# Top-32 attention and a highway layer on one core: the 32nd score joins the maximum that gives the top score and the threshold

## The chip, the cores and the metric

The kernel runs on one core of a Trainium2 chip. A core has five engines with a queue each: TensorE (PE in the profile; PEld is its weight load), VectorE (DVE), ScalarE (ACT), GpSimd (POOL) and SyncE (SP), and 16 DMA engines that all queues share. The engines run side by side and meet at semaphores: an instruction waits at the head of its queue until what it reads has been written, and what stands behind it on that queue waits too. The metric is the device time of one execution in microseconds (us); the median of the runs counts.

## The reference, cut to what matters

Eight batches of eight heads, 576 queries and keys of 64 numbers each. Of each row of 576 scores the 32 largest stay, and the softmax goes over those; the result, with the heads side by side, goes through a highway layer.

```python
scores = scale * np.matmul(q, k.transpose(0, 1, 3, 2))          # (8, 8, 576, 576)
kth = np.partition(scores, -32, axis=-1)[..., -32:-31]
scores = np.where(scores >= kth, scores, -1000000000.0)
attn = np.exp(scores - np.max(scores, axis=-1, keepdims=True))
attn = attn / (np.sum(attn, axis=-1, keepdims=True) + 1e-09)
x = (attn @ v), heads side by side                              # (4608, 512)
H = np.maximum(x @ w_h, 0.0)
T = 1.0 / (1.0 + np.exp(-(x @ w_t + b_t)))
out = T * H + (1.0 - T) * x
```

## The kernel before, in words

**Units and pairs.** A unit is 128 rows of 576 scores: 128 queries of one head, or the last 64 queries of two heads. Two units make a pair, and there are 288 units and 144 pairs. `step(i)` is called for 143 pairs, in order; the order of the instructions on each queue is the order of the code (`manual_schedule`), written out by hand. A start (`begin`) and an end (`finish`) stand around the steps.

**How a row finds its 32nd score.** TensorE writes the scores of a pair into PSUM (`xs`). VectorE takes the eight largest of each of six segments of 96 (`segs`, L353, twelve MAX8 for a pair) into `cand`, a tile of 8 groups of 8 for each unit. `refine` (L358 to L388) narrows these 48 down. Elementwise maxima and minima of neighbouring segments (`high`, `low`, L366 and L368), a sign change (`neg`, L370), and four MAX8 over 24 (L373, L376) give two sorted lists for each unit. A joint operation on them (L378) writes eight numbers into column 1 of `cand`, and one `tensor_reduce` (L382) takes the maximum of columns 0 and 1 over the groups. The first is the row's top score, the second a threshold THR with about 24 scores above it. Both go to `wall`, a table with a row for each unit.

ScalarE then makes a mask of the scores above THR and counts them (`mask_count`, L397, count in `csum`). TensorE adds the mask to the scores in PSUM (L410), so that the scores above THR fall out, and VectorE takes the eight largest of what remains (`below`, L420, two MAX8 over 576) into `wall`. With the threshold itself these are nine numbers (NPK), of which the count tells which one is the 32nd: `hits` (L426, VectorE) sets a flag of nine for the one whose place fits the count, `pick_a` (L436, GpSimd) multiplies the flags with the nine numbers, and `pick_b` (L439, VectorE) adds the nine products, of which all but one are zero. The 32nd of a pair is stored two rows further on in `wall`, in the row of the next pair.

**What uses it.** `biases` (L391, GpSimd) turns the top score of pair i+1 and the 32nd of pair i into two biases (`be`). For the first unit of a pair ScalarE makes a filter `r` from its bias (L443), which VectorE joins with the exponentials `e` (`keep_min`, L450). For the second GpSimd compares the scores with the 32nd (`above_one`, L454), and VectorE multiplies (`keep_mul`, L460). Where GpSimd has too much to do, VectorE does both in one instruction (L465). The results `ep` are transposed by a DMA (L481), and TensorE multiplies them with the values.

**The order around the change.** In `step(i)` VectorE does: twelve `segs` of pair i+1, two `below` of pair i, `high` and `low` of pair i+1, `hits` of pair i, `neg` and the four small MAX8 of pair i+1, `pick_b` of pair i, the joint operation (L378), `keep_min` of pair i-1, the `tensor_reduce` (L382), for some steps two small instructions for the highway layer, and `keep_mul` of pair i-1. GpSimd does `above_one`, one operation of the highway layer (`do_work`), `pick_a`, then the DMAs that it issues itself, and `biases`, which is made to wait for `keep_mul`. GpSimd's DMAs are, one in most steps and two in some: an accumulating add into `s1` (`do_add`, L694), a cast of `x` into `xb` (L582), or a load of values or weights (L176 to L222). What an add or a cast fills is stored or transposed by SyncE two steps later. ScalarE's masks of pair i+1 close the step.

Of the kernel before, what the change touches and what calls it, by code (L numbers as in the profile page):

```python
# [10 lines left out]
ALU = mybir.AluOpType  # L11
FP32 = mybir.dt.float32
# [6 lines left out]
NSEG = 6  # L19
RANK = 24  # L20
ABOVE = -(1.0 + 2.0**-23)
# [5 lines left out]
def kernel(  # L27
# [10 lines left out]
    nc = tc.nc  # L38
    P = nc.NUM_PARTITIONS
# [26 lines left out]
    NU = len(units)  # L66
# [3 lines left out]
    consts = ctx.enter_context(tc.tile_pool(name="consts", bufs=1))  # L70
# [23 lines left out]
    NPK = TOP_K - RANK + 1  # L94
# [1 line left out]
    for jj in range(NPK):  # L96
        nc.vector.memset(pidx[:, jj : jj + 1], S - 2.0 * (TOP_K - jj))

    TOP, THR, KTH = 0, 1, NPK + 1
    wall = consts.tile([P, NU + 2, NPK + 2], FP32)  # L100
    fac = consts.tile([P, 2, 2], FP32)
    nc.vector.memset(fac[:, :, 0], -scale)
# [6 lines left out]
        nc.vector.memset(en[:, 0, :, 0:1], 3.0e38)  # L109
        ends.append(en)  # L110
    csum = consts.tile([P, NU], FP32)
    nc.vector.memset(wall[:, 0:2, KTH : KTH + 1], 0.0)

    def kth(u):
        return wall[:, u + 2, KTH : KTH + 1]
# [6 lines left out]

    cands = []
    for i in range(4):
        cand = consts.tile([P, 2, 8, 8], FP32, name=f"cand{i}")
        nc.vector.memset(cand[:, :, NSEG:, 0:1], -3.0e38)
        cands.append(cand)
    NM = 4
    masks = []
# [228 lines left out]
    def refine(g, cand):  # L358
        u0, u1 = pairs[g][0], pairs[g][1] + 1
        en = ends[g % NE]  # L360
        one = cand[:, :, 0:NSEG:2, :]
        two = cand[:, :, 1:NSEG:2, ::-1]
        high = cpool.tile([P, 2 * HALF], FP32, name="high")
        low = cpool.tile([P, 2 * HALF], FP32, name="low")
        neg = cpool.tile([P, 2 * HALF], FP32, name="neg")
        nc.vector.tensor_tensor(high[:].rearrange("p (s k r) -> p s k r", s=2, r=8), one, two, ALU.max)  # L366
        yield
        nc.vector.tensor_tensor(low[:].rearrange("p (s k r) -> p s k r", s=2, r=8), one, two, ALU.min)  # L368
        yield
        nc.vector.tensor_scalar(neg[:], high[:], -1.0, None, ALU.mult)  # L370
        yield
        for s in range(2):
            nc.vector.max(en[:, 0, s, 1:9], low[:, s * HALF : (s + 1) * HALF])  # L373
            yield
        for s in range(2):
            nc.vector.max(en[:, 1, s, 0:8], neg[:, s * HALF : (s + 1) * HALF])  # L376
            yield
        nc.vector.scalar_tensor_tensor(  # L378
            out=cand[:, :, :, 1], in0=en[:, 1, :, 0:8], scalar=-1.0, in1=en[:, 0, :, 0:8], op0=ALU.mult, op1=ALU.min
        )  # L380
        yield
        nc.vector.tensor_reduce(  # L382
            wall[:, u0:u1, TOP : THR + 1],
            cand[:, :, :, 0:2].rearrange("p s r k -> p s k r"),
            mybir.AxisListType.X,
            ALU.max,
        )
        yield  # L388

    def biases(g):  # L390
        return nc.gpsimd.tensor_tensor(be[:, g], wall[:, 2 * g : 2 * g + 2, TOP : KTH + 1 : KTH - TOP], fac[:], ALU.mult)  # L391

# [22 lines left out]
        return e  # L417

    def below(u, ps):
        nc.vector.max(wall[:, u, THR + 1 : KTH], ps)  # L420


    def hits(pair):
        u0, u1 = pair[0], pair[1] + 1
        hit = cpool.tile([P, 2, NPK], FP32, name="hit")
        nc.vector.tensor_tensor(  # L426
            hit[:],
            pidx[:].unsqueeze(1).to_broadcast([P, 2, NPK]),
            csum[:, u0:u1].unsqueeze(2).to_broadcast([P, 2, NPK]),
            ALU.is_equal,  # L430
        )
        return hit

    def pick_a(pair, hit):
        u0, u1 = pair[0], pair[1] + 1
        nc.gpsimd.tensor_tensor(hit[:], hit[:], wall[:, u0:u1, THR:KTH], ALU.mult)  # L436

    def pick_b(pair, hit):
        nc.vector.tensor_reduce(wall[:, pair[0] + 2 : pair[0] + 4, KTH], hit[:], mybir.AxisListType.X, ALU.add)  # L439
# [263 lines left out]
    st = {}  # L703
# [71 lines left out]
    def step(i):  # L775
        j = i - 3
        live = i < NG
        prev = 0 <= i - 1 < NG
        back = 0 <= j < NG
        nxt = i + 1 < NG  # L780
        b, k_in = divmod(i, SPB)
        last_steps = i >= NG - 8
        nb = len(stages)
        if i == 3 or nb < B and i >= (nb - 2) * SPB + 16 > 16 - 1 and not to_prep:
            stages[nb] = stage_tiles()
            todo_kq.extend(loads_kq(nb, *stages[nb]))
        if live and b + 1 < B:
            if k_in == 3:
                todo_v.extend(loads_v(b + 1, vbs[(b + 1) % 2]))
            if k_in == (1 if b else 7):  # L790
                preps[b + 1] = prep_alloc(kds[(b + 1) % 2])
                parts = [(hp, part) for hp in range(NP) for part in range(2)]
                parts[2:2] = [(0, 7), (0, 8)]
                to_prep.extend((b + 1, *part) for part in parts)
        layers.extend(ready)
        ready.clear()
        if live:
            pr = pairs[i]
            for s in range(2):
                mask_add(st[i]["ps"][s], st[i]["m"][s], s)  # L800
        if prev:
            pu, ps_ = pairs[i - 1], st[i - 1]
            ps_["r"] = [above(pu[0], ps_["sc"][0])]
            ps_["r"].append(above_one(pu[1], ps_["sc"][1]) if len(pool_work) < (3 if last_steps else 5) else None)
        if late:
            late.pop(0)()
        if back:
            back_pv(j)
            back_xs(j)
            st.pop(j)  # L810
        spare(8 if i + 2 >= NG or units[pairs[i + 2][0]][1] < nfull or po["n"] else 3)
        ev = prep_filler() if to_prep and (i <= SPB or (len(to_prep) > 15 - k_in or len(layers) > 2) and i % 2) else None
        do_work(nc.gpsimd, 2 * dm if prev and ps_["r"][1] is None else dm)
        segs(i + 1, 2 * NSEG)
        if live:
            below(pr[0], st[i]["ps"][0])
            below(pr[1], st[i]["ps"][1])
        if live:
            st[i]["e"] = [expo(pr[0], st[i]["sc"][0])]
        if nxt:  # L820
            copy_both(i + 1)
        if ev:
            ev()
        if i + 2 < NG:
            start_scores(i + 2)
        if layers and (last_steps or i <= SPB or kind[0] or not to_prep):
            kind[0] = False
            late.append(layers.pop(0)())
        elif i > SPB:
            kind[0] = True  # L830
            piece = prep_filler()
            if piece:
                late.append(piece)
        spare(4 if late else 10)
        if live:
            st[i]["e"].append(expo(pr[1], st[i]["sc"][1]))
            pass
        ra = refine(i + 1, st[i + 1]["cand"]) if nxt else iter(())

        def masked(s):  # L840
            if not prev:
                return None
            u = pu[s]
            if ps_["r"][s] is not None:
                ep, ins = (keep_min, keep_mul)[s](u, ps_["e"][s], ps_["r"][s])
            else:
                ep, ins = keep(u, ps_["sc"][s], ps_["e"][s])
            ps_["et"][s] = transposes(ep)
            return ins

        for _ in range(2):
            next(ra, None)
        if live:
            hit = hits(pr)
            pick_a(pr, hit)
        added = bool(adds or casts)
        if adds:
            do_add(i)
        elif casts:
            turns.append((i + 2, casts.pop(0)()))  # L860
        elif todo_v:
            todo_v.pop(0)()
        if todo_v and (i < 5 or added and i <= SPB):
            todo_v.pop(0)()
        for _ in range(5):
            next(ra, None)
        if live:
            pick_b(pr, hit)
        next(ra, None)
        masked(0)  # L870
        for _ in ra:
            pass
        scaling = norms.pop(0)() if norms else iter(())
        next(scaling, None)
        last = masked(1)
        if live:
            after(biases(i + 1), last)
        next(scaling, None)
        if nxt:
            masks_of(i + 1)  # L880
        while turns and turns[0][0] <= i and len(flying) < 2:
            turns.pop(0)[1]()
        while stores and stores[0][0] <= i:
            stores.pop(0)[1]()
        for _ in range(min(2, len(todo_kq))):
            todo_kq.pop(0)()
# [56 lines left out]
    def finish():  # L943
# [49 lines left out]
        hit = hits(pr)  # L993
        ep, _ = keep_min(pu[0], old["e"][0], relu)
        old["et"][0] = transposes(ep)
        nc.vector.tensor_tensor(hit[:], hit[:], wall[:, pr[0] : pr[1] + 1, THR:KTH], ALU.mult)
        pick_b(pr, hit)
        x2 = xps.tile([P, 3 * BANK], FP32, tag="x", name="xs")
        cur["et"] = [etpool.tile([P, nck, P], BF16, name="et") for s in range(2)]
# [13 lines left out]
        yb = xs_of(nfull, 0, n)  # L1013
        project(bank(x1, 0), ya["qt"], ya["xT"], wh, False)
        do_work(nc.vector, NG * dm)
        nc.vector.scalar_tensor_tensor(cond[:], wall[:, 0:NU, THR + 1], ABOVE, wall[:, 0:NU, THR], ALU.mult, ALU.add)
        while stores:
            stores.pop(0)[1]()
        sure(2, cond[:], 1.0)
# [119 lines left out]
```

## Time and profile before

| | |
|---|---|
| median of 3 runs | 806.73 us (806.29 to 807.61) |
| the profiled execution's own time | 806.17 us |
| its span, first to last instruction | 804.5 us |
| VectorE busy | 772.8 us, 96% |
| ScalarE busy | 757.2 us, 94% |
| TensorE busy | 686.7 us, 85% |
| GpSimd busy | 559.9 us, 70% |
| granted TensorE clock, mean | 0.996 |

The profile is that of one execution. A group of instructions is printed as line, engine, operation, output and inputs with their shapes, count; then the busy time in us and the mean in ns of one; then the idle time of the engine just ahead of them, and what ended it. A timeline row gives the start in us from the span's start, the duration in us, engine, line, operation, and in brackets the idle time before it with what ended it. Instructions on an engine overlap a little in the records: the next one starts before the one before it has ended, so what an instruction takes of its queue's time is the distance from its start to the next start.

### The profile page before, as it was taken

To read this page: it belongs to the slowest core of one execution; us is meant where nothing else is said; L and a number is where in the kernel's file an instruction comes from. 1 tells how busy PE (TensorE), PEld (TensorE's weight loads), DVE (VectorE), ACT (ScalarE), POOL (GpSimd) and SP (SyncE) were. 2 spreads that over 40 slices of the span, in tenths; PEclk is the share of its full clock that TensorE was granted. 3 is DMA by queue.
4 is the path that set the end of the run, shared out by engine and by line. 5 is a ranking of instruction groups with operands and counts; after the bars stand their busy time and mean duration, and the time that the engine had idled before them with its cause. 6 is when DMAs were issued, how large, how long until landed. Compare 5 with 4: busy or idle time off the path is not lost.

```text
span 804.5 us, 20583 instructions
## 1 busy us (share of the span) xinstructions
PE 686.7 (85%) x6369; PEld 494.7 (61%) x6459; DVE 772.8 (96%) x4020; ACT 757.2 (94%) x1401; POOL 559.9 (70%) x712
## 2 busy tenths in 40 slices
PE   7889998888888888888987889888888888988884
PEld 5666766566666666566665666666666566665662
DVE  5999999999999999999999999999999999999996
ACT  5999999999999999999999999999999999999984
POOL 2666867777777767777767776777776777766750
PEclk9999999999999999999999999999999999999998
DMA  6789968996799667998669766898767996555653
GB/s 121 87 137 159 134 116 140 141 143 93 140 152 148 108 96 137 154 131 125 102 135 159 125 113 107 150 156 126 112 121 136 160 124 109 90 106 110 108 90 88
DMA packets 346359, 100.37 MB, mean 125 GB/s; under 512 B 330624, under 2 KB 338432, under 8 KB 346240
## 3 DMA queue, kind: packets, MB, share of 16 engines
q1 hardware_dynamic: 291024, 79.16, 54.1%
q0 software_dynamic: 53536, 19.34, 22.6%
q8 instruction: 53, 0.87, 0.4%
q10 hardware_dynamic: 1680, 0.46, 0.3%
q14 instruction: 66, 0.54, 0.2%
HBM read 31.72 MB, written 9.44 MB: 51 GB/s over the span
## 4 chain that ended last, share of the span: by engine, by line
ACT 37%; DVE 32%; PE 23%; DMA 4%; issue 3%; SPq 1%; another core or an unknown queue 0%; DVEq 0%; ACTq 0%
ACT m L397 15%; DVE wall L420 12%; DVE cand L353 9%; ACT e L416 7%; ACT sc L348 6%; PE pso L278 5%; ACT r L443 4%; PE xs L309 4%; PE xs L326 3%; DVE ep L450 3%; DMA xT<-xb 3%; PE fp L522 3%; PE xs L410 3%; PE pso L494 2%; ACT xs L508 2%
## 5 line engine op out<-in xcount | busy, mean ns | idle before, releaser
L353 DVE MAX8 cand<-xs 128x8 f32<-128x96 f32 x1728 | 297.5, 248 | 11.4 <-PE xs L335 6.2
L278 PE MATMUL pso<-cst,ident_b 128*128 128x252 bf16 x1841 | 246.8, 272 | 42.8 <-ACT xs L508 40.4
L454 POOL TENSOR_SCALAR ro<-sc,wall 128x576 bf16<-128x576 f32 x135 | 232.8, 1724 | 0.0
L416 ACT ACTIVATE e<-sc,be 128x576 bf16<-128x576 f32 x288 | 226.5, 787 | 0.1
L278 PEld LDWEIGHTS <-ident_b 128*128 128x128 bf16 x1841 | 173.4, 98 | 81.4 <-issue 49.5
L420 DVE MAX8 wall<-xs 128x8 f32<-128x576 f32 x288 | 204.3, 751 | 5.6 <-PE xs L410 3.5
L309 PE MATMUL xs<-kT,qT 64*128 64x256 f32 x1024 | 145.3, 400 | 30.6 <-DVE high L366 26.2
L348 ACT COPY sc<-xs 128x1152 f32<-128x1152 f32 x144 | 161.0, 1118 | 0.7 <-DVE cand L353 0.6
L309 PEld LDWEIGHTS xs<-kT,qT 64*128 64x128 f32 x1024 | 93.0, 186 | 61.3 <-issue 37.6
L397 ACT ACTIVATE m<-xs,wall 128x576 int8<-128x576 f32 x144 | 107.4, 746 | 18.2 <-DVE wall L382 17.1
L436 POOL TENSOR_TENSOR hit<-hit,wall 128x18 f32<-128x18 f32 x143 | 32.4, 227 | 121.2 <-DVE hit L426 114.0
L397 ACT ACTIVATE m<-sc,wall 128x576 int8<-128x576 f32 x144 | 111.4, 773 | 0.0
L443 ACT ACTIVATE r<-sc,be 128x576 bf16<-128x576 f32 x143 | 109.9, 769 | 0.0
L410 PE MATMUL xs<-m,ident_b 128*128 128x512 bf16 (+1 forms) x512 | 92.7, 274 | 17.3 <-ACT m L397 15.2
L494 PEld LDWEIGHTS <-et 128*128 128x128 bf16 (+1 forms) x1600 | 68.6, 100 | 19.2 <-issue 3.5
L391 POOL TENSOR_TENSOR be<-wall,fac 128x4 f32<-128x4 f32 x144 | 29.2, 203 | 72.5 <-DVE ep L460 53.7
L410 PEld LDWEIGHTS <-ident_b 128*128 128x128 bf16 x576 | 51.7, 97 | 44.8 <-issue 24.1
L494 PE MATMUL pso<-vb,et 128*128 128x65 bf16 (+1 forms) x1600 | 74.4, 194 | 4.2 <-DMA et<-ep 0.3
L450 DVE TENSOR_TENSOR ep<-e,r 128x576 bf16<-128x576 bf16 x143 | 64.6, 452 | 0.2 <-ACT r L443 0.2
L318 PEld LDWEIGHTS xs<-kd,qT 128*128 128x128 f32 x256 | 38.1, 188 | 42.5 <-issue 42.1
L318 PE MATMUL xs<-kd,qT 128*128 128x128 f32 x256 | 62.5, 326 | 0.0
L460 DVE TENSOR_TENSOR ep<-e,ro 128x576 bf16<-128x576 bf16 x135 | 60.7, 449 | 0.0
(127 smaller groups left out, 1028.9 us busy)
## 6 DMA issues: line engine op xcount, KB each, us to landing
kin<-in_k_dram SPq DMA_DIRECT2D x64, 128.0 KB, 2.9
qin<-in_q_dram SPq DMA_DIRECT2D x62, 128.0 KB, 3.1
out_dram<-s SPq DMA_DIRECT2D x30, 256.0 KB, 2.8
s<-h POOLq DMA_DIRECT2D x29, 256.0 KB, 4.0
et<-ep SPq DMA_TRANSPOSE x286, 3.3
xb<-x POOLq DMA_DIRECT2D x30, 128.0 KB, 3.0
vb<-in_v_dram POOLq DMA_DIRECT2D x28, 128.0 KB, 4.8
vb<-in_v_dram POOLq DMA_DIRECT2D x24, 64.0 KB, 3.1
```

The lines of the kernel that those rows point to most:

```text
L278: nc.tensor.matmul(po["t"][:, 4 * DE : BANK], ident_b[:], cst[:, 0 : BANK - 4 * DE], start=True, stop=True, skip_group_check=True,)
L309: nc.tensor.matmul(ps[:, mo + n0 : mo + n0 + 256], qT[r : r + D, hp, qs : qs + P], kT[r : r + D, hp, n0 : n0 + 256], start=(n0 == 0), stop ...
L318: nc.tensor.matmul(ends, qT[:, hp, qs : qs + P], kd[:, hp, :], start=True, stop=True)
L348: nc.scalar.copy(sc[:], both)
L353: nc.vector.max(cand[:, s, :], sc[:, s * SEG : (s + 1) * SEG])
L397: nc.scalar.activation(m1[:].bitcast(I8)[:, 1 : 2 * S : 2], ps, AF.Sign, bias=wall[:, u, THR : THR + 1], scale=ABOVE, accum_out=csum[:, u ...
L410: nc.tensor.matmul(ps[:, s0:s1], ident_b[:], m1[:, s0:s1], start=False, stop=True, skip_group_check=True)
L416: nc.scalar.activation(e[:], sc, AF.Exp, bias=tb(u), scale=scale)
L420: nc.vector.max(wall[:, u, THR + 1 : KTH], ps)
L443: nc.scalar.activation(r[:], sc, AF.Relu, bias=eb(u), scale=BIGK)
L454: nc.gpsimd.tensor_scalar(r[:], sc, kth(u), None, ALU.is_ge)
L494: nc.tensor.matmul(pso[r0 : r0 + ql, col : col + DE], ets[s][:, c, gi * P2 : gi * P2 + ql], vb[:, h, vc, :], start=(c == 0), stop=(c == nc ...
```

## The change

The 32nd becomes a third column of the joint maximum. `cand` grows from 8 to 9 groups, and its columns are now 0 the top score, 1 the 32nd (KTH), 2 the threshold (THR). GpSimd's product of flags and numbers is written straight into column 1 of `cand` of pair i+1, and the `tensor_reduce` takes the maximum over nine groups of three columns where it took two columns over eight groups. The sum `pick_b` goes out of the step (it stays in `finish`). `wall` has its columns in the order 0 top, 1 32nd, 2 threshold, 3 to 10 the eight below.

Two things move. `hits` goes from between `low` and `neg` to behind the fourth small MAX8, and the product goes with it; and the DMAs that GpSimd issues in a step now stand ahead of the product in its queue.

```diff
-    TOP, THR, KTH = 0, 1, NPK + 1
+    TOP, KTH, THR, LOW = 0, 1, 2, 3
...
-    nc.vector.memset(wall[:, 0:2, KTH : KTH + 1], 0.0)
...
-        cand = consts.tile([P, 2, 8, 8], FP32, name=f"cand{i}")
-        nc.vector.memset(cand[:, :, NSEG:, 0:1], -3.0e38)
+        cand = consts.tile([P, 2, NPK, 8], FP32, name=f"cand{i}")
+        nc.vector.memset(cand[:, :, NSEG:, :], -3.0e38)
...
-            out=cand[:, :, :, 1], in0=en[:, 1, :, 0:8], scalar=-1.0, in1=en[:, 0, :, 0:8], op0=ALU.mult, op1=ALU.min
+            out=cand[:, :, 0:8, THR], in0=en[:, 1, :, 0:8], scalar=-1.0, in1=en[:, 0, :, 0:8], op0=ALU.mult, op1=ALU.min
...
-            wall[:, u0:u1, TOP : THR + 1],
-            cand[:, :, :, 0:2].rearrange("p s r k -> p s k r"),
+            wall[:, u0:u1, TOP:LOW],
+            cand[:, :, :, TOP:LOW].rearrange("p s r k -> p s k r"),
...
-    def pick_a(pair, hit):
-        u0, u1 = pair[0], pair[1] + 1
-        nc.gpsimd.tensor_tensor(hit[:], hit[:], wall[:, u0:u1, THR:KTH], ALU.mult)
+    def pick(pair, pen, cand):
+        nc.gpsimd.tensor_tensor(cand[:, :, :, KTH], pen[:], wall[:, pair[0] : pair[1] + 1, THR:], ALU.mult)
...
-        for _ in range(2):
-            next(ra, None)
-        if live:
-            hit = hits(pr)
-            pick_a(pr, hit)
         added = bool(adds or casts)
         if adds:
             do_add(i)
...
-        for _ in range(5):
+        for _ in range(7):
             next(ra, None)
         if live:
-            pick_b(pr, hit)
+            pick(pr, hits(pr), st[i + 1]["cand"])
         next(ra, None)
         masked(0)
```

The other lines of the diff only follow the new columns (`biases`, `below`, and `finish`).

More of the change, by code (lines that the diff above doesn't have):

```diff
@@ L390, in biases @@
     def biases(g):
-        return nc.gpsimd.tensor_tensor(be[:, g], wall[:, 2 * g : 2 * g + 2, TOP : KTH + 1 : KTH - TOP], fac[:], ALU.mult)
+        return nc.gpsimd.tensor_tensor(be[:, g], wall[:, 2 * g : 2 * g + 2, TOP:THR], fac[:], ALU.mult)
     def mask_count(u, ps):
@@ L419, in below @@
     def below(u, ps):
-        nc.vector.max(wall[:, u, THR + 1 : KTH], ps)
+        nc.vector.max(wall[:, u, LOW:], ps)
     def hits(pair):
@@ L995, in finish @@
         old["et"][0] = transposes(ep)
-        nc.vector.tensor_tensor(hit[:], hit[:], wall[:, pr[0] : pr[1] + 1, THR:KTH], ALU.mult)
+        nc.vector.tensor_tensor(hit[:], hit[:], wall[:, pr[0] : pr[1] + 1, THR:], ALU.mult)
         pick_b(pr, hit)
@@ L1015, in finish @@
         do_work(nc.vector, NG * dm)
-        nc.vector.scalar_tensor_tensor(cond[:], wall[:, 0:NU, THR + 1], ABOVE, wall[:, 0:NU, THR], ALU.mult, ALU.add)
+        nc.vector.scalar_tensor_tensor(cond[:], wall[:, 0:NU, LOW], ABOVE, wall[:, 0:NU, THR], ALU.mult, ALU.add)
         while stores:
```

## The prediction, made before the changed kernel ran

> **What bounds the kernel now.** I read the page first: the shares of the engines, the chain that ended last, the costliest groups. Then one step of VectorE and of GpSimd in the timeline, then the rows of single lines.
>
> ```profile
> PE 686.7 (85%) x6369; PEld 494.7 (61%) x6459; DVE 772.8 (96%) x4020; ACT 757.2 (94%) x1401; POOL 559.9 (70%) x712
> ACT 37%; DVE 32%; PE 23%; DMA 4%; issue 3%; SPq 1%; another core or an unknown queue 0%; DVEq 0%; ACTq 0%
> L353 DVE MAX8 cand<-xs 128x8 f32<-128x96 f32 x1728 | 297.5, 248 | 11.4 <-PE xs L335 6.2
> L420 DVE MAX8 wall<-xs 128x8 f32<-128x576 f32 x288 | 204.3, 751 | 5.6 <-PE xs L410 3.5
> L397 ACT ACTIVATE m<-xs,wall 128x576 int8<-128x576 f32 x144 | 107.4, 746 | 18.2 <-DVE wall L382 17.1
> L436 POOL TENSOR_TENSOR hit<-hit,wall 128x18 f32<-128x18 f32 x143 | 32.4, 227 | 121.2 <-DVE hit L426 114.0
> ```
>
> VectorE stands still for 11.4 + 5.6 = 17 us in its two largest groups and is busy for the rest of the steps: a step lasts as long as its VectorE instructions, one behind the other. ScalarE is close behind (94%), and its masks wait for VectorE's `tensor_reduce` (L382). GpSimd has room: it idles 121.2 us ahead of its product, 0.85 us a step, because the flags come late. So the change is priced on VectorE: each 0.01 us on its queue is 1.4 us over 143 steps, and whatever VectorE waits for GpSimd counts in full.
>
> One step of VectorE from `high` on, then GpSimd's two small operations of it:
>
> ```profile
> 409.57 0.19 DVE L366 TENSOR_TENSOR high<-cand 128x48 f32<-128x48 f32 x1
> 409.68 0.20 DVE L368 TENSOR_TENSOR low<-cand 128x48 f32<-128x48 f32 x1
> 409.80 0.17 DVE L426 TENSOR_TENSOR hit<-pidx,csum 128x18 f32<-128x18 f32 x1
> 409.88 0.18 DVE L370 TENSOR_SCALAR neg<-high 128x48 f32<-128x48 f32 x1
> 409.98 0.26 DVE L373 MAX8 en<-low 128x8 f32<-128x24 f32 x2
> 410.16 0.26 DVE L376 MAX8 en<-neg 128x8 f32<-128x24 f32 x2
> 410.33 0.16 DVE L439 TENSOR_REDUCE wall<-hit 128x2 f32<-128x18 f32 x1
> 410.44 0.19 DVE L378 SCALAR_TENSOR_TENSOR cand<-en 128x16 f32<-128x16 f32 x1
> 410.54 0.45 DVE L450 TENSOR_TENSOR ep<-e,r 128x576 bf16<-128x576 bf16 x1
> 410.90 0.21 DVE L382 TENSOR_REDUCE wall<-cand 128x4 f32<-128x32 f32 x1
> 411.03 0.45 DVE L460 TENSOR_TENSOR ep<-e,ro 128x576 bf16<-128x576 bf16 x1
> ```
>
> ```profile
> 410.04 0.23 POOL L436 TENSOR_TENSOR hit<-hit,wall 128x18 f32<-128x18 f32 x1 [1.66 <-DVE hit L426]
> 411.56 0.20 POOL L391 TENSOR_TENSOR be<-wall,fac 128x4 f32<-128x4 f32 x1 [1.28 <-DVE ep L460]
> ```
>
> The reader sees three delays here. The product starts 0.24 us after the flags do (409.80 to 410.04). It ends at 410.27, and the sum that needs it starts 0.06 later, when VectorE comes to it anyway. And small instructions cost by their distances: the sum holds VectorE for 0.11 us (410.33 to 410.44), though it is recorded with 0.16.
>
> **The change part by part.**
>
> *The sum goes.* 143 x 0.11 = 15.7 us less on VectorE.
>
> *The `tensor_reduce` grows* from 32 to 54 elements. The two MAX8 groups give the price of an element, (751 - 248) / (576 - 96) = 1.05 ns, so 22 of them are 0.023 us, 3.3 us in all. The other end: the reduce over 32 is recorded with 0.21, the sum over 18 with 0.16, which is 3.6 ns an element, 0.08 us and 11.4 us. I take 0.023, as the distances behind the two differ by only 0.02 (0.11 and 0.13).
>
> Together 12.4 us less, 0.087 us a step, if nothing new waits.
>
> *The `tensor_reduce` now waits for GpSimd's product.* This is the new wait, and behind it on VectorE stand `keep_mul` and the next step; ScalarE's masks and `biases` wait for its result too. Count from the start of the flags in their new place. The joint operation (L378) starts 0.08 later (as `neg` did, 409.80 to 409.88), `keep_min` 0.10 after that, the reduce 0.36 after that: it is due at 0.54. The product starts at 0.24 and takes 0.23; with 0.06 to VectorE the reduce may start at 0.53. On paper this just fits, and then the wait costs nothing.
>
> But the product's neighbours are others now. Before, it ran beside the small MAX8, which read one tensor; now it runs beside the joint operation and `keep_min`, which read two. The trace shows what that does, in both directions:
>
> ```profile
> 781.79 1.53 DVE L465 SCALAR_TENSOR_TENSOR ep<-sc,wall,e 128x576 bf16<-128x576 f32 x2
> 782.68 0.71 POOL L391 TENSOR_TENSOR be<-wall,fac 128x4 f32<-128x4 f32 x1 [1.64 <-DVE ep L465]
> L391 POOL TENSOR_TENSOR be<-wall,fac x144: 188/193/711, 13.8 to 782.7; 128x4 f32<-128x4 f32 x144
> 283.76 1.27 POOL L610 TENSOR_TENSOR s<-h,x 128x512 f32<-128x512 f32 x1 [0.81 <-ACT h L609]
> 284.44 0.66 DVE L366 TENSOR_TENSOR high<-cand 128x48 f32<-128x48 f32 x1
> L366 DVE TENSOR_TENSOR high<-cand x144: 183/190/655, 12.5 to 780.3; 128x48 f32<-128x48 f32 x144
> ```
>
> `biases` takes 0.193 us (the median). The one time it met a two-input VectorE operation (the second of the two L465, which ends at 783.32) it took 0.71 and ended at 783.39, 0.06 after that operation. `high` takes 0.19, and 0.66 where GpSimd's addition was running when it came: it ended at 285.10, 0.07 after the addition's end (285.03). One of the two stands until the other is through.
>
> So I expect the product to stand until `keep_min` is through. `keep_min` ends at 0.08 + 0.10 + 0.45 = 0.63. The product ends 0.06 later as `biases` did, and up to 0.03 more for its larger size (227 against 193 ns): 0.69 to 0.72. With 0.06 to VectorE the reduce starts at 0.75 to 0.78, 0.21 to 0.24 late. If the product comes first instead and `keep_min` stands, `keep_min` moves by nearly the product's 0.23, and the reduce with it: the same. I take 0.22, 31.5 us over 143 steps. The low end of this cost is nothing (the 0.53 above).
>
> The Trainium skill, "SBUF — State Buffer", section "SBUF: two separate sides", has this as a rule: VectorE with two SBUF inputs and GpSimd reading SBUF share a port pair, and whichever starts first holds it for its whole instruction. The two rows above agree with it; by the rule alone the sum would be the one taken here, by the median of 193 ns alone it would be the one without a wait. That the rule also holds for the bf16 form of `keep_min` no row of this profile shows.
>
> *The flags move behind five VectorE instructions*, 0.44 us later (410.33 - 409.80 is 0.53, less their own 0.09). Those five need nothing of them, and only GpSimd waits for them. The product in the new place writes into `cand` after `high` and `low` have read it, so no wait comes from there. Free.
>
> *GpSimd's DMAs move ahead of the product.* Each DMA instruction of the step now delays the product if GpSimd has no time for it:
>
> ```profile
> L694 POOL DMA_DIRECT2D s<-h x36 | 33.2, 922 | 9.3 <-POOL hit L436 9.3
> L187 POOL DMA_DIRECT2D vb<-in_v_dram x28 | 27.2, 972 | 7.5 <-issue 7.5
> L582 POOL DMA_DIRECT2D xb<-x x37 | 23.1, 624 | 10.4 <-POOL hit L436 10.4
> 521.77 1.26 POOL L610 TENSOR_TENSOR s<-h,x 128x512 f32<-128x512 f32 x1
> 523.27 0.17 DVE L426 TENSOR_TENSOR hit<-pidx,csum 128x18 f32<-128x18 f32 x1
> 524.46 0.98 POOL L187 DMA_DIRECT2D vb<-in_v_dram  x1 [0.72 <-issue]
> ```
>
> GpSimd has on average 0.85 + 0.44 = 1.29 us for it. An add takes 0.92 and stands 9.3 / 36 = 0.26 before, a column load 0.97 + 0.27, a cast 0.62 + 0.28. Casts fit; the 64 adds and column loads fit by 0.05 to 0.11 on average, so about half of them will not. The step at 521.77 shows a bad one: GpSimd is free at 523.03, the load would be issued at 523.03 + 0.72 + 0.98 = 524.73, while the product is due at 523.27 + 0.44 + 0.24 = 523.95; late by 0.78. For 32 late steps I estimate 0.3 us, of which the 0.22 of the port wait is paid already where the lateness is small: some 0.15 each on top, 5 us (ends: nothing, if the waits ahead of the issues vanish with the product gone from in front of them, and the 10 us of the whole 0.3). What the DMAs bring comes up to a microsecond earlier, and nobody waits for it: adds and casts are picked up by SyncE two steps later, in an order that stays.
>
> *What is given back.* Where VectorE comes 0.13 us later to its segments, its waits for TensorE there shrink. Of the 17 us I take 3.5, a fifth; at most all of it.
>
> *The rest.* The larger fill of `cand` lies in the start, before any scores are there. `finish` changes only columns.
>
> Sum: - 15.7 + 3.3 + 31.5 + 5 - 3.5 = + 20.6 us. Against the profiled execution's own 806.17 us (span 804.5) that is 826.8. The median shown, 806.73, stands 0.07% above this execution, which is inside what can be told here: under 0.2% is no difference for a measurement of this kernel. I say 827.
>
> **The rivals.**
>
> *The product slips through beside `keep_min`* (the bf16 multiplication leaves GpSimd its reads, or the product gets in before it). For it: no row shows GpSimd computing beside L450 or L460. Against it: in both rows above the second comer stood to the end. Then the reduce is due when the product is ready, VectorE saves 12.4 us, and late GpSimd issues give back between nothing and 10 us; of what is left, ScalarE at 94% may keep a few us. 794 to 808, likeliest 801. It decides at the wait: below 0.087 us a step on the mean, late issues included, the kernel is faster.
>
> *GpSimd's issues are the larger wait.* If 32 steps are late as the one at 521.77, the reduce starts 0.77 late there, 0.55 beyond the port wait: 17.6 us in place of 5, 839 us. Against it: a wait of 0.72 before the issue is the longest sort, the mean is 0.27.
>
> *The joint operation waits for the product too*, because both write into `cand`, in columns that lie in turn. It would start at 0.53 after the flags and not at 0.08, 0.45 x 143 = 64 us, less 12.4: 858 us. Against it:
>
> ```profile
> 0.86 1.61 SPq L160 DMA_DIRECT2D kin<-in_k_dram  x2
> L160 SPq DMA_DIRECT2D kin<-in_k_dram x64: 540/583/1339, 0.9 to 640.6; - x64
> DMA to landing us min/median/max: 2.4/3.0/5.3
> ```
>
> Two loads into columns of `kin` that lie in turn start within 1.61 us, though none of these lands in under 2.4: the second does not wait for the first.
>
> **How the numbers follow.** The forecast has 0.66, with its own range 813 to 840 (a wait of 0.19 to 0.24 us, a reduce that grows by nothing to 0.08, late issues from 2 to 10 us). The product that slips through has 0.22, larger issue waits 0.08, the joint operation's wait 0.04. The range 801 to 840 leaves out half of the second, half of the third and the last, 0.19. Faster 0.18: two thirds of the slip-through, and the forecast's low tail with a smaller port wait, 0.03. Same 0.04, out of the slip-through. Slower 0.78.
>
> **What would show it.** Right: the group of the product on GpSimd has a mean near 0.45 us in place of 0.227; the `tensor_reduce` has an idle time of some 35 us ahead of it, ended by GpSimd's `cand`, and starts in the timeline about 0.06 us after the product's end, in almost every step; its distance to the next instruction is near 0.15; L439 has one instruction left; VectorE's idle time grows and its busy time falls by about 12 us. Late issues show as product starts more than 0.3 us behind the flags, right after an L694 or L187. Wrong: a product of 0.23 us beside `keep_min` means there is no port wait; an idle time ahead of L378 means the joint operation waits; a reduce idle time above 50 us with product starts behind DMA rows means that the issues are the larger wait.

## The result, and the profile after

The changed kernel takes 832.23 us (median of 5 runs, 830.11 to 833.15) against 806.29 for the kernel before in the same comparison: a ratio of 1.0312, 95% interval 1.0294 to 1.0331, slower by 26 us. The profiled execution took 832.76 us with a span of 831.1, 26.6 longer than before.

The page of the changed kernel: engine shares, the chain that ended last, and the groups that answer to those shown of before.

```profile
PE 698.9 (84%) x6369; PEld 497.0 (60%) x6459; DVE 786.3 (95%) x3876; ACT 762.2 (92%) x1401; POOL 589.9 (71%) x712
DVE 34%; PE 23%; ACT 19%; POOL 15%; issue 5%; DMA 3%; SPq 0%; another core or an unknown queue 0%; POOLq 0%; DVEq 0%; ACTq 0%
L352 DVE MAX8 cand<-xs 128x8 f32<-128x96 f32 x1728 | 296.5, 247 | 5.2 <-PE xs L334 2.6
L419 DVE MAX8 wall<-xs 128x8 f32<-128x576 f32 x288 | 203.5, 747 | 5.0 <-PE xs L409 3.4
L396 ACT ACTIVATE m<-xs,wall 128x576 int8<-128x576 f32 x144 | 107.1, 743 | 39.8 <-DVE wall L381 37.5
L434 POOL TENSOR_TENSOR cand<-hit,wall 128x18 f32<-128x18 f32 x143 | 70.6, 494 | 75.8 <-DVE hit L425 71.0
```

GpSimd was not in the chain before and now holds 15% of it. Its product has gone from 227 to 494 ns. ScalarE's first mask waits 37.5 us for the `tensor_reduce` where it waited 17.1. VectorE waits less than before at its segments (5.2 against 11.4). And VectorE is busy for longer, 786.3 against 772.8 us, with 144 instructions fewer: an instruction that has started and stands until another engine is through is counted as busy.

The timeline of the changed kernel, an ordinary step of VectorE from `high` on (the MAX8 rows are called top-eights from here on), and GpSimd's product of that step:

```profile
424.05 0.19 DVE L365 TENSOR_TENSOR high<-cand 128x48 f32<-128x48 f32 x1
424.15 0.20 DVE L367 TENSOR_TENSOR low<-cand 128x48 f32<-128x48 f32 x1
424.27 0.19 DVE L369 TENSOR_SCALAR neg<-high 128x48 f32<-128x48 f32 x1
424.39 0.27 DVE L372 MAX8 en<-low 128x8 f32<-128x24 f32 x2
424.58 0.25 DVE L375 MAX8 en<-neg 128x8 f32<-128x24 f32 x2
424.75 0.16 DVE L425 TENSOR_TENSOR hit<-pidx,csum 128x18 f32<-128x18 f32 x1
424.86 0.19 DVE L377 SCALAR_TENSOR_TENSOR cand<-en 128x16 f32<-128x16 f32 x1
424.96 0.45 DVE L448 TENSOR_TENSOR ep<-e,r 128x576 bf16<-128x576 bf16 x1
425.53 0.26 DVE L381 TENSOR_REDUCE wall<-cand 128x6 f32<-128x54 f32 x1
```

```profile
424.99 0.51 POOL L434 TENSOR_TENSOR cand<-hit,wall 128x18 f32<-128x18 f32 x1 [1.69 <-DVE hit L425]
```

The product starts 0.24 us after the flags, as it always did, and ends at 425.50, 0.09 after `keep_min` (425.41). The `tensor_reduce` starts 0.03 later, 0.57 after `keep_min`'s start, where it was 0.36 before.

A second kind of step, with a column load (one of the loads of values, L186) that GpSimd issues while VectorE comes to `neg`; GpSimd's row follows:

```profile
152.16 0.18 DVE L365 TENSOR_TENSOR high<-cand 128x48 f32<-128x48 f32 x1
152.27 0.20 DVE L367 TENSOR_TENSOR low<-cand 128x48 f32<-128x48 f32 x1
152.38 0.67 DVE L369 TENSOR_SCALAR neg<-high 128x48 f32<-128x48 f32 x1
152.50 0.56 DVE L372 MAX8 en<-low 128x8 f32<-128x24 f32 x2
153.09 0.27 DVE L375 MAX8 en<-neg 128x8 f32<-128x24 f32 x2
```

```profile
152.09 0.98 POOL L186 DMA_DIRECT2D vb<-in_v_dram  x1
```

`high` and `low` run through while the load is issued. `neg` stands until 153.05, and the load's issue ends at 153.07; the two top-eights behind it stand too. In the trace 28 of the 144 `neg` do so, 23 beside a column load. The line of `neg` before and after (count, minimum, median and maximum in ns):

```profile
L370 DVE TENSOR_SCALAR neg<-high x144: 174/180/185, 12.7 to 780.6; 128x48 f32<-128x48 f32 x144
L369 DVE TENSOR_SCALAR neg<-high x144: 173/183/681, 12.5 to 806.3; 128x48 f32<-128x48 f32 x144
```

Not every `neg` that meets an issue stands: 89 started while GpSimd was issuing a DMA, and 61 of them ran through. The 28 started 0.29 to 0.57 us into the issue. Beside a column load all 23 that started in this stretch stood; beside a cast none of 34 did, whenever it started.

Since VectorE sets the pace, the whole difference can be laid out on its queue. Each instruction is taken from its start to the start of the next, summed over the trace, in us:

| VectorE, start to next start | before | after | difference |
|---|---|---|---|
| `keep_min` (L450, L448), up to the reduce | 52.7 | 83.2 | +30.5 |
| the sum (L439) | 16.7 | 0.6 | -16.1 |
| `neg` and the two top-eights over `low` | 39.6 | 52.0 | +12.4 |
| the `tensor_reduce` (L382, L381) | 18.0 | 24.6 | +6.6 |
| the flags (L426, L425) | 12.9 | 17.1 | +4.3 |
| `keep_mul`, `reciprocal`, segments (with their waits for TensorE) | 362.1 | 351.1 | -11.0 |

These come to + 26.7; the spans differ by 26.6.

### The profile page after: what moved, and what is told of

The parts are those of the page before. It is cut to its first block, busy times and chain, and to the rows that moved or that the text cites. A ratio compares the mean times of both kernels' runs of the same rounds, so it can differ in the third digit from the quotient of the medians.

```text
span 831.1 us, 20580 instructions
## 1 busy us (share of the span) xinstructions
PE 698.9 (84%) x6369; PEld 497.0 (60%) x6459; DVE 786.3 (95%) x3876; ACT 762.2 (92%) x1401; POOL 589.9 (71%) x712
## 4 chain that ended last, share of the span: by engine, by line
DVE 34%; PE 23%; ACT 19%; POOL 15%; issue 5%; DMA 3%; SPq 0%; another core or an unknown queue 0%; POOLq 0%; DVEq 0%; ACTq 0%
DVE wall L419 16%; ACT m L396 13%; DVE cand L352 6%; POOL cand L434 5%; PE pso L277 4%; POOL ro L452 4%; PE xs L409 3%; PE pso L492 3%; PE xs L325 3%; PE xs L308 3%; PE fp L520 3%; POOL h L622 3%; DVE wall L381 2%; DVE neg L369 2%; POOL s L692 2%
## 5 line engine op out<-in xcount | busy, mean ns | idle before, releaser
L396 ACT ACTIVATE m<-xs,wall 128x576 int8<-128x576 f32 x144 | 107.1, 743 | 39.8 <-DVE wall L381 37.5
L434 POOL TENSOR_TENSOR cand<-hit,wall 128x18 f32<-128x18 f32 x143 | 70.6, 494 | 75.8 <-DVE hit L425 71.0
L409 PE MATMUL xs<-m,ident_b 128*128 128x512 bf16 (+1 forms) x512 | 96.3, 274 | 31.9 <-ACT m L396 29.3
L448 DVE TENSOR_TENSOR ep<-e,r 128x576 bf16<-128x576 bf16 x143 | 64.6, 452 | 0.2 <-ACT r L441 0.2
```

The source lines that it names most:

```text
L396: nc.scalar.activation(m1[:].bitcast(I8)[:, 1 : 2 * S : 2], ps, AF.Sign, bias=wall[:, u, THR : THR + 1], scale=ABOVE, accum_out=csum[:, u ...
L409: nc.tensor.matmul(ps[:, s0:s1], ident_b[:], m1[:, s0:s1], start=False, stop=True, skip_group_check=True)
L434: nc.gpsimd.tensor_tensor(cand[:, :, :, KTH], pen[:], wall[:, pair[0] : pair[1] + 1, THR:], ALU.mult)
```

## The experiments

Two waits are in sight, both of VectorE and GpSimd with each other (the expectations call them port waits), and one puzzle: the sum is gone with its 16 us, and little of that seems to arrive. Each part of the change is undone or done alone, and each suspected wait is taken away by itself.

**Undone: the DMAs back behind the product.**

```diff
-        (GpSimd's DMAs)
         for _ in range(7):
             next(ra, None)
         if live:
             pick(pr, hits(pr), st[i + 1]["cand"])
+        (GpSimd's DMAs)
```

> The changed kernel with GpSimd's DMAs put back behind the product; everything else as changed. Theory (two port waits: the product stands behind keep_min in every step, some 30 us; the sign change neg stands behind a DMA that GpSimd is issuing in some 28 steps, some 11 us): neg falls back to 0.18 us in every step, the product stays at 0.50, the tensor_reduce still starts 0.57 after keep_min, and the time falls from 832 to 819-826 us. Rival (the DMA issues cost only by making the product late, 1 us in all): 830-832 us, and neg keeps its long ones.

Measured: 825.94 us, ratio 1.0231 (1.0216 to 1.0245). First the lines of `neg` and `high` in this kernel, with count, minimum, median and maximum in ns; then the group of the product:

```profile
L369 DVE TENSOR_SCALAR neg<-high x144: 176/182/189, 12.3 to 801.2; 128x48 f32<-128x48 f32 x144
L365 DVE TENSOR_TENSOR high<-cand x144: 182/188/971, 12.1 to 801.0; 128x48 f32<-128x48 f32 x144
```

```profile
L434 POOL TENSOR_TENSOR cand<-hit,wall 128x18 f32<-128x18 f32 x143 | 72.1, 505 | 167.1 <-DVE hit L425 158.2 <-DVE cand L377 7.5 <-DMA xT<-xb 1.3
```

No `neg` stands any more, and 6 us are back. The place of the DMAs is one of the two costs. Part of the gain is lost again: in 27 steps, 7 before, `high` stands behind one of GpSimd's highway operations (4.9 us more on VectorE than before). That GpSimd's round ends later with the issues behind the product is the likely reason.

**One part alone: the joint maximum, flags and DMAs at their old places.**

```diff
-        (GpSimd's DMAs)
-        for _ in range(7):
+        for _ in range(2):
             next(ra, None)
         if live:
             pick(pr, hits(pr), st[i + 1]["cand"])
+        (GpSimd's DMAs, then five other parts of refine)
```

> The joint maximum alone: flags and product at their old place, between low and neg, and the DMAs behind the product. Theory: beside the small top-eights, which read one tensor, the product takes 0.23 us, the tensor_reduce starts 0.37 after keep_min with no wait, the sum's 16 us are gone and the larger reduce takes 5 to 7 back: 795-801 us, ratio 0.985-0.994. Rival (the product is slow because it writes every eighth number of cand): the product takes 0.50 here too, though the reduce may not notice it.

Measured: 810.41 us, ratio 1.0042 (1.0030 to 1.0054), slower than before by 3 us. The product takes 230 ns here, so a slow strided write is out, and the reduce waits for nothing. But the 16 us do not arrive. The timeline of this kernel shows where they went:

```profile
410.72 0.26 DVE L372 MAX8 en<-low 128x8 f32<-128x24 f32 x2
410.90 0.25 DVE L375 MAX8 en<-neg 128x8 f32<-128x24 f32 x2
411.19 0.19 DVE L377 SCALAR_TENSOR_TENSOR cand<-en 128x16 f32<-128x16 f32 x1
```

The two top-eights end at 411.15, and the joint operation that reads them starts 0.03 to 0.04 after that end. Before, the sum stood between them, the joint operation started 0.04 before the sum's end, and yet it started just as long after the end of the last top-eight: the median is 0.034 us in both kernels. Over the trace the last top-eight now holds VectorE for 16.1 us more: just what the sum had taken. The larger reduce, 5.6 us more, makes this kernel slower. My theory failed on the time; the next run asks whether the joint operation waits for its inputs or for the product.

**The sum taken out of the kernel before.**

```diff
-    nc.vector.memset(wall[:, 0:2, KTH : KTH + 1], 0.0)
+    nc.vector.memset(wall[:, :, KTH : KTH + 1], 0.01)
...
-        if live:
-            pick_b(pr, hit)
```

> The kernel before with the sum pick_b left out of the steps (the 32nd is a constant 0.01 there, so the rows kept are not the reference's). With the joint maximum alone the sum's 16 us were gone and VectorE stood 0.11 us longer between the last small top-eight and L378 in every step. Theory (L378 must wait for the end of the top-eight that it reads; the sum only filled this time): L378 starts 0.20 after the last top-eight, 0.03 after its end, and the time stays within 3 us of before. Rival (there L378 waited for the product, which writes the same tile): here the product writes a tile of its own, L378 follows 0.09 after the top-eight, and the time falls by 10 to 16 us.

Measured: 810.08 us, ratio 1.0039 (1.0025 to 1.0053). One instruction less in each step, and not a microsecond gained. Its timeline:

```profile
410.40 0.25 DVE L376 MAX8 en<-neg 128x8 f32<-128x24 f32 x2
410.69 0.19 DVE L378 SCALAR_TENSOR_TENSOR cand<-en 128x16 f32<-128x16 f32 x1
```

The same hole, with the product in a tile of its own. So the joint operation waits for the end of the top-eight in front of it, and the sum had lain in that wait for nothing. (Why this run is 3.3 us above before, a little more than the 3 us that the theory allowed, isn't settled; its largest difference on VectorE beside the sum and its hole is 2.9 us more at the segments.)

**One part alone: the flags behind the last small top-eight, in the kernel before.**

```diff
-        for _ in range(2):
+        for _ in range(7):
             next(ra, None)
         if live:
             hit = hits(pr)
             pick_a(pr, hit)
         (GpSimd's DMAs)
-        for _ in range(5):
-            next(ra, None)
-        if live:
-            pick_b(pr, hit)
         next(ra, None)
         masked(0)
+        if live:
+            pick_b(pr, hit)
```

> The kernel before with one part of the change alone: flags and product behind the fourth small top-eight; the sum, which needs the product, goes between keep_min and the tensor_reduce; the DMAs stay behind the product. Theory: the product takes 0.50 beside keep_min, the sum starts 0.57 after keep_min in place of 0.37, 29 us over the steps, less 5 to 12 us that other waits give back: 822-834 us. Rival (only a product into cand is slow): product 0.23, within 5 us of before.

Measured: 829.39 us, ratio 1.0263 (1.0247 to 1.0279). The product and the sum that waits for it:

```profile
L436 POOL TENSOR_TENSOR hit<-hit,wall 128x18 f32<-128x18 f32 x143 | 71.9, 503 | 168.9 <-DVE hit L426 156.3 <-DVE cand L378 8.2 <-DMA out_dram<-s 1.8
```

```profile
413.77 0.45 DVE L450 TENSOR_TENSOR ep<-e,r 128x576 bf16<-128x576 bf16 x1
414.34 0.17 DVE L439 TENSOR_REDUCE wall<-hit 128x2 f32<-128x18 f32 x1
```

503 ns and 0.57 us, with the product in `hit` as it always was. The place of the product is the cause, and neither `cand` nor the joint maximum.

**One part alone: the DMAs ahead of the product, in the kernel before.**

```diff
             hit = hits(pr)
-            pick_a(pr, hit)
         (GpSimd's DMAs)
+        if live:
+            pick_a(pr, hit)
```

> The kernel before with one part of the change alone: GpSimd's DMAs ahead of its product, flags and sum where they were. Theory: neg stands behind a DMA issue in 25 to 35 steps, 0.2 to 0.5 us each, and the time rises by 7 to 12 us to 813-819 us; the product stays at 0.23. Rival (the DMA's place costs nothing by itself): within 0.2% of before. Rival (late product): neg stays at 0.18 and the sum waits for GpSimd.

Measured: 833.59 us, ratio 1.0331 (1.0316 to 1.0346). Both the wait of the theory and that of the second rival are seen, and the rival's is the larger, so the time lies far above the 813 to 819 us of the theory. The line of `neg`, then VectorE's longest wait (us in total, times, longest):

```profile
L370 DVE TENSOR_SCALAR neg<-high x144: 171/178/587, 12.2 to 806.6; 128x48 f32<-128x48 f32 x144
```

```profile
DVE wall L439 <- POOL hit L436: 18.6, 36, 1.4
```

`neg` stands here too, in 31 steps (with the top-eights behind it 7.1 us more than before). And with the flags early, GpSimd has too little time for the issues: the sum waits, and the last top-eight up to the sum takes 28.8 us more. In the changed kernel, with the flags 0.44 later, late products are rare: what goes beyond 0.6 us from `keep_min` to the reduce comes to 1.1 us in all.

**One wait taken away: `keep_min` with one input.**

```diff
-        return ep, nc.vector.tensor_tensor(ep[:, pad : pad + S], e[:], r[:], ALU.min)
+        return ep, nc.vector.max(junk[:], e[:, 0:ONE])          # ONE = 288
```

> The changed kernel, with keep_min replaced by a top-eight over 288 numbers of e, which holds VectorE as long (0.37 us to the next start) and reads one tensor; the filtered exponentials of the first unit of each pair are left out (zeros go into the transposes). Theory: the product takes 0.23 us and the tensor_reduce starts about 0.37 after the instruction in keep_min's place, so most of the 30 us go: 800-808 us. Rival (a slow strided write): product 0.50, reduce 0.57 behind, 830 us or so.

Measured: 812.23 us, ratio 1.0054 (1.0038 to 1.0070). The timeline of one step and the group of the product:

```profile
423.09 0.45 DVE L450 MAX8 junk<-e 128x8 bf16<-128x288 bf16 x1
423.46 0.23 DVE L383 TENSOR_REDUCE wall<-cand 128x6 f32<-128x54 f32 x1
```

```profile
L436 POOL TENSOR_TENSOR cand<-hit,wall 128x18 f32<-128x18 f32 x143 | 37.2, 260 | 79.0 <-DVE hit L427 74.8 <-DVE cand L379 3.9
```

An instruction of the same length and one tensor less to read, and the product is back to 0.22 (its median), with the reduce 0.37 behind. Some 20 us go with it, fewer than expected (800 to 808 us); `neg` still stands in 32 steps here. The bf16 form of `keep_min` does hold GpSimd's product off, which no row had shown before the change. The stand-in differs in more than one way, though: it also writes 8 numbers where `keep_min` writes 576. That the second input is what counts is not shown apart from that.

**The other wait taken away: `neg` with two inputs.**

```diff
-        nc.vector.tensor_scalar(neg[:], high[:], -1.0, None, ALU.mult)
+        nc.vector.tensor_tensor(neg[:], high[:], minus[:], ALU.mult)
```

> The changed kernel with the sign change neg made as a product of two tensors (high times a tile of -1), where it was one tensor times a constant. In the changed kernel neg stands to the end of a DMA that GpSimd is issuing, while high and low, which have two inputs, go through beside the same DMA. Theory (only the one-input form needs the second port pair against a DMA issue): neg's long ones vanish and the time falls by 7 to 11 us, to 821-826 us, as with the DMAs behind the product. Rival (VectorE stands behind GpSimd's issues at this point whatever the form): neg or the next instruction keeps its 0.65 in some 28 steps, 831-834 us.

Measured: 822.76 us, ratio 1.0198 (1.0182 to 1.0213). All 144 `neg` lie between 197 and 210 ns, although 23 of them started 0.29 to 0.57 us into a column load, as many as in the changed kernel:

```profile
L371 DVE TENSOR_TENSOR neg<-high,minus x144: 197/205/210, 12.6 to 796.8; 128x48 f32<-128x48 f32 x144
```

It is the one-input form of `neg` that stands behind a DMA issue. A slower form without the wait gains 9 us.

**Both waits taken away.**

```diff
     (keep_min as a top-eight over 288 numbers of e)
-        (GpSimd's DMAs)
         (refine, flags, product)
+        (GpSimd's DMAs)
```

> The changed kernel with both port waits taken away: the DMAs behind the product, and a top-eight over 288 numbers of e in place of keep_min (the filtered exponentials of the first unit of each pair are left out). Theory (what is left of the change is worth next to nothing, since the sum had filled a wait, and the flags do so now): 800-808 us. Rival (the prediction's own sum without its wait, 12 us saved): 791-797 us.

Measured: 809.11 us, ratio 1.0030 (1.0020 to 1.0039). The groups of the product, the reduce and `high`:

```profile
L436 POOL TENSOR_TENSOR cand<-hit,wall 128x18 f32<-128x18 f32 x143 | 32.9, 230 | 165.5 <-DVE hit L427 158.4 <-DVE cand L379 7.2
L383 DVE TENSOR_REDUCE wall<-cand 128x6 f32<-128x54 f32 x144 | 33.4, 232 | 0.2 <-POOL cand L436 0.2
L367 DVE TENSOR_TENSOR high<-cand 128x48 f32<-128x48 f32 x144 | 37.9, 263 | 0.0
```

Neither wait is left, and the kernel is still no faster than before; the time is just above the theory's 800 to 808 us. On VectorE's queue the sum gives 16.4 us, the larger reduce takes 4.2, the flags, `neg` and the top-eights over `low` in their new order take 8.0, and `high`, which now stands behind GpSimd's highway operations in 43 steps, 9.1. Without the last item some 4 us would remain of the prediction's 12.4, by this sum; no run shows it.

No version came out ahead of the kernel before: there the sum fills the hole ahead of the joint operation, and the flags another one ahead of `neg`.

## Why the prediction was right, and where its terms were not

827 us were forecast and 832 measured; slower by 2.5% was forecast, 3.1% came. The step that decided was right. Other terms were off: the sum with the flags by 11 us, the two waits with the DMAs by 2.7, and what is given back by 7.5 the other way. That these errors cancel in part, so that the total is off by 6 us only, is luck.

- **The product stands until `keep_min` is through**: right. 0.22 us a step and 31.5 us were taken; the median measured is 0.205, and the whole 30.5 us, late products included. The product ended 0.086 after `keep_min` (0.06 to 0.09 was said). The reduce followed 0.034 after the product and not 0.06. An instruction of the same length with one input in `keep_min`'s place took the wait away, and moving the flags alone brought it about.
- **The sum goes, 15.7 us less**: the row is there, 16.1, but the step "143 x 0.11 less on VectorE" failed. The distance of 0.11 was read as the sum's cost, and it was the filling of a wait that stays. Taken out alone it gained nothing (810.08 us). In the changed kernel the flags fill the hole. The rows in the prediction already show it: the top-eights end at 410.16 + 0.26 = 410.42, and the joint operation that reads them starts at 410.44.
- **The flags move, "Free"**: failed. They had filled a hole of the same kind ahead of `neg` (3.7 us more for `neg` and the top-eights over `low` with the DMAs behind) and take 4.3 more at their new place, since the joint operation still waits for the top-eight. Sum gone, reduce grown, flags moved: the runs give - 16.1 + 6.6 + 8.0 = - 1.5 us, where the prediction had - 12.4.
- **The reduce grows by 3.3 us**: 6.6, inside the two ends; 0.046 us a step.
- **The DMAs ahead, 5 us of late products**: 9.8 us, inside the ends of 0 and 10, but mostly for another reason. Late products cost 1.1: 7 products started more than 0.3 us behind the flags, where 32 were expected. What was missed is that VectorE stands behind an issue: 52.0 - 43.3 (the same three instructions with the DMAs behind) = 8.7 us. The issues' waits are shorter ahead of the product: a column load stood 7.5 us in all before and 0.2 now.
- **Given back, 3.5 us**: 11.0. VectorE comes later to its segments in every step, and its waits for TensorE shrink: the idle time ahead of the segments fell from 11.4 to 5.2 us. The rest of the 11.0 is not broken down.
- **The rivals.** The product that slips through would have needed what the run with one input did, and even that is not faster than before. The joint operation does wait, but for the top-eight and not for the product. Larger issue waits are real where the flags stay early (833.59 us), and the changed order avoids them.
- **The signs.** Right: product near 0.45 (0.494), the reduce behind the product in almost every step. Wrong: an idle time of 35 us ahead of the reduce (18.9, since idle is counted from `keep_min`'s end and the lost overlap of 0.08 a step is not in it), a distance of 0.15 from the reduce to the next start (0.17), and a busy time 12 us lower (13.5 higher).

## What to carry to other kernels

Before pricing a removed instruction by its distance, look at whether the one behind it reads what the one ahead of it writes: then the distance may be filling, and it comes back as a wait. Before moving work between VectorE and GpSimd, list what runs on the other engine at the new place, and how many SBUF inputs each has. A DMA that GpSimd issues counts as such a neighbour too, for a one-input instruction such as `neg`.

## What the runs showed of the hardware that was not expected

- In these runs a VectorE instruction that waits for another one's result starts 0.034 us after that one's end, whether something stands between the two or not: the joint operation did so behind the last top-eight with nothing between, with the sum and with the flags (medians). Where nothing waited, starts lay 0.04 to 0.085 ahead of the preceding end. For a top-eight over 24 numbers that is 0.20 us to the next start in place of 0.084.
- A one-input fp32 instruction from SBUF to SBUF (`neg`) can stand until GpSimd is through with a DMA issue: 0.67 us in place of 0.18 beside a column load. It depends on when it starts: all 23 that started 0.29 to 0.57 us into a column load stood nearly to the issue's end, and none beside a cast; four stood beside an accumulating add, to some 0.28 us ahead of its end. With two inputs `neg` did not stand in 23 such places (210 ns at most). `high` and `low`, fp32 with two inputs, ran through as well, but only 2 and 5 of them started in that stretch. Against a GpSimd addition it was the two-input form that stood (`high`, up to 0.66 before the change). The Trainium skill, "SBUF — State Buffer", section "SBUF: two separate sides", names as takers of the port pair that VectorE shares with GpSimd the operations in a two-port mode, which a `tensor_scalar` such as `neg` can enter, and those with two SBUF inputs, the latter only against a GpSimd operation that reads SBUF. The runs fit these kinds; whether `neg` ran in such a mode no run here shows. By the same section the first comer keeps the pair for its whole instruction; the 61 of 89 `neg` that ran through during an issue do not fit that, if the pair counts as held from an issue's recorded start to its end.
